# The end of the expert stage and the value products behind it: another list for the fillers, other engines for the copies, the taps of two batches moved among the output tiles

## The chip, the core and the metric

One core of a Trainium2 chip runs the whole program. The metric is device time in microseconds (us). A profile holds one execution, with the busy time of TensorE (PE for its matmuls, PEld for its weight loads), VectorE (DVE), ScalarE (ACT), GpSimd (POOL) and the DMA queue of SyncE (SP).

## The reference, cut to what matters

```python
# stage 1: attention, batch 4, 8 heads, 1152 positions, 64 wide, queries pooled by 2
x = softmax(pool(q) @ k.T / 8) @ v              # -> (4, 576, 512)
# stage 2: four experts, top 2 of 4, causal attention inside each
for e in range(4):
    y = softmax(causal(x @ wq[e] @ (x @ wk[e]).T / 8)) @ (x @ wv[e]) @ wo[e]
    out += (e among the top two) * gate_weight * y
# stage 3: a causal convolution of 5 taps makes the gate of a value product
gate_pre = sum(conv_w[k] * shifted(out, k) for k in range(5))
final = (sigmoid(gate_pre) * (out @ w_val)) @ w_out
```

All of it is float32. The kernel splits operands into a high and a low part in the matmul's reduced float32 format, so that a product is three matmuls: high by high, low weights by high, high weights by low.

## The kernel before

**Order.** All instructions are issued in an order written by hand; the engines run their own queues in order, and semaphores join them. Stage 2 is a loop over `n = 0..41`. Step `n` issues the scores of one tile (batch `b`, expert pair `g`, query block `i`, in the order i = 1, 3, 2, 4, 0, so that five steps make a pair and ten a batch). Two steps later (`LAG = 2`) the same tile's probabilities are transposed (`transp2`). A tile goes through: scores on PE (`scores2`), mask and row minimum on DVE, exponential on ACT (`expo2`), a reciprocal on DVE and a scaling on GpSimd (`norm2`, L850 or L855), transposes on PE, copies out of PSUM by `evac`. When the last tile of a pair is transposed, `av2` multiplies with the values; it is put at place 1 of the list `fill`.

**Fillers.** Between these, `pop` takes PE work from `fill`: projections of the next batch (`proj`, twelve matmuls), value and router products (`vgate`), output products of a batch (`mix`, six matmuls of 288 columns), and from n = 35 on fourteen of the sixteen value products of batches 0 and 1 (`raws`, six matmuls of 288 columns each, L779). How many are popped in a step follows from estimated costs and a `budget`. What a filler leaves for other engines is put on `late2` and issued at the next pop: for `raws` the copy out of PSUM, by `evac`. `evac` sends every other copy to ACT (L862) and to DVE (L864); its counter `turn` begins at 0 and serves `transp2` too, all through stage 2.

**Taps.** `mix` writes its rows to `x2` and, scaled with the last tap's weight, to `gp`, both on ACT (L937, L938). `conv` then hangs four taps a tile row on the list `rides`, DVE instructions of 576 columns (L215); each pop issues one, and each step one more, three a step at most (`room`).

**Behind the loop.** What is left of `fill` and the last two `raws` run, then `gate_all(0)` (sigmoids on ACT, L795, four multiplications on DVE, L1136), the eight `mix` halves of batch 3 with splits of the gated rows of batch 0 between them (`spread`, L790 on ACT and L791 on DVE), then the 18 output tiles `final(i, t)` of twelve matmuls (L1120): pair 0 is batches 0 and 1, pair 1 batches 2 and 3. `VF` says how many value products of batches 2 and 3 (`values`) follow each tile; each is multiplied with its gate on DVE (L1127) and split. `step` issues one entry, the leftovers of the one before and one or two taps.

**PSUM.** Projections, transposes, `mix`, `raws` and `av2` share four banks of `ps_m`. A bank comes free when its copy has run. Scores have two tiles of their own.

Of the kernel before, what the change touches and what calls it, by code (L numbers as in the profile page):

```python
# [12 lines left out]
AF = mybir.ActivationFunctionType  # L13
# [7 lines left out]
def tile_kernel(ctx, tc, q, k, v, w_gate, wq, wk, wv, wo, w_val, conv_w, w_out, wo_t, q0, k0, out):  # L21
# [751 lines left out]
    def value(yhs, b, m, hf, then):  # L773

        qsl = slice(hf * HQ, (hf + 1) * HQ)
        ps = ps_m.tile([P, 512], F32, name="a")
        ops = [(wi, yi, g) for g in range(EP) for wi, yi in THREE]
        for o, (wi, yi, g) in enumerate(ops):
            pe.matmul(ps[:, 0:HQ], lhsT=wf[:, g, wi, m * P:(m + 1) * P], rhs=yhs[b, g][:, yi, qsl], start=o == 0, stop=o == len(ops) - 1)  # L779
        late2.append(lambda: then(ps[:, 0:HQ], m, qsl))  # L780
# [16 lines left out]
    with ExitStack() as s2l:  # L797
# [56 lines left out]
                    dve.tensor_tensor(out=sm[rs, 0:1], in0=sm[rs, 0:1], in1=gw[rs, 4, 2 * g + e:2 * g + e + 1], op=ALU.mult)  # L854
                pool.tensor_tensor(out=p[:, 0:SQ], in0=p[:, 0:SQ], in1=sm[:, 0:1].to_broadcast([P, SQ]), op=ALU.mult)  # L855

        turn = [0]

        def evac(dst, src):
            turn[0] += 1  # L860
# [63 lines left out]
        def mix(b, yhs):  # L924

            box = {}

            def half(m, hf):
                if hf == 0:
                    box[m] = ((x2_p if m < 2 else x2b_p).tile([P, SQ], F32, name="x2"), o_p.tile([P, SQ], F32, name="gp")) if b < B - 1 else (end3["x2"][m], end3["gp"][m])  # L930
                x2, gp = box[m]
                qsl = slice(hf * HQ, (hf + 1) * HQ)
                ps = ps_m.tile([P, 512], F32, name="a")
                ops = [(wi, yi, g) for g in range(EP) for wi, yi in THREE]
                for o, (wi, yi, g) in enumerate(ops):
                    pe.matmul(ps[:, 0:HQ], lhsT=wos[wi][:, g, m * P:(m + 1) * P], rhs=yhs[g][:, yi, qsl], start=o == 0, stop=o == len(ops) - 1)
                act.activation(x2[:, qsl], ps[:, 0:HQ], AF.Copy)  # L937
                act.activation(gp[:, qsl], ps[:, 0:HQ], AF.Copy, scale=cw[:, m, KC - 1:KC])  # L938
                if hf == 1:
                    late2.append(lambda: rides.extend(conv(b, m, x2, gp)))  # L940

            return [(0.74, lambda m=m, hf=hf: half(m, hf)) for m in range(KT) for hf in range(2)]
# [7 lines left out]
            return steps  # L950

        VG, FD, IN, FL, PEND, PN = 5, 1, 1, 2.6, 7, 3
        GM, VF = (0, 1, 2, 3), (0, 0, 0, 3, 1, 2, 2, 2, 2, 2, 2)
        RD = (1, 0, 1, 1, 1)
        ORDER = (1, 3, 2, 4, 0)
        steps = [(b, g, i) for b in range(B) for g in range(EP) for i in ORDER]
        LAG = 2
        WORK = [(0.21, 0.22), (0.43, 0.44), (0.64, 0.65), (0.85, 0.87), (0.96, 0.55)]
# [37 lines left out]
        for n in range(len(steps) + LAG):  # L996
            if n < len(steps):
                b, g, i = s = steps[n]
                if n % 5 == 0:
                    pts[b, g] = (pt_p2.tile([P, 4, 2, SQ], F32, name="pt"), pt_p2.tile([R64, 2, R64], F32, name="pt4"))  # L1000
                    if g == 0 and b:
                        fill += proj(xh[b], 1, (lambda: xh.update({3: load2(3)})) if b == 2 else None)
                        if b == B - 1:
                            fill.append((0, lambda: late2.append(begin3)))
                    if n == 10 * B - 5:
                        buf = [f(c2.tile([P, 2, SQ], F32R, name=f"k20{i}")) for i in range(2)]
                        bufs = [c2.tile([P, SQ + R64], F32R, name=f"q20{i}") for i in range(2)]
                        v2 = v_p.tile([P, 5, ED + E], F32, name="v2").rearrange("p t c -> p (t c)")
                        first3["raw"] = [[buf[t // 2][:, t % 2] for t in range(KT)], [f(bufs[t])[:, 0:SQ] if t < 2 else v2[:, (t - 2) * SQ:(t - 1) * SQ] for t in range(KT)]]
                        raws = [(0.74, lambda i=i, m=m, hf=hf: value(yhs, i, m, hf, lambda ps, m, qsl: evac(first3["raw"][i][m][:, qsl], ps))) for i in range(2) for m in range(KT) for hf in range(2)]  # L1010
                        fill += raws[0:14]
                    if b == 0 and g == 1:
                        buf = y0_p.tile([P, EP, 2, SQ], F32R, name="y0")
                        yhs.update({(0, i): buf[:, i] for i in range(EP)})
                    if b == 1 and g == 0:
                        buf = y12_p.tile([P, 2, EP, 2, SQ], F32R, name="y12")
                        yhs.update({(1 + j, i): buf[:, j, i] for j in range(2) for i in range(EP)})
                if n % 10 == 5 and b + 1 < B:
                    fill += proj(xh[b + 1], 0)
                if n % 10 == VG and b + 1 < B:  # L1020
                    v2s[b + 1], gws[b + 1], vg = vgate(xh[b + 1])
                    fill += vg
                if n == 0:
                    fill += proj(xh[0], 1)
                if n == FD:
                    fill += [(2.6, lambda g=g: fold(g)) for g in range(EP)]
# [2 lines left out]
            own = [ahead(m) for m in range(n, n + left)]  # L1029
            budget = max(FL, (sum(c for c, _ in fill) + (PEND if 10 <= n and n % 10 < PN else 0) + sum(own)) / left) - own[0]  # L1030

            room = [3]

            def ride():
                if urgent:
# [19 lines left out]
                t += pop()  # L1055
            if n < len(steps):
                scores2(s)
            if fill:
                t += pop(RD[n % 5])
            else:  # L1060
                flush()
            if n >= LAG:
                b1, g1, i1 = steps[n - LAG]
# [8 lines left out]
                expo2(s)  # L1072
            if n == 0:
                flush()
            while fill and t < budget:
                t += pop()
            ride()
            if n == 9:
                xh[2] = load2(2)
            if n in (12, 22):  # L1080
# [13 lines left out]
                    rides.pop(0)()  # L1094

        CL = 2
        while len(fill) > 6:
            step(fill.pop(0)[1])
    s2.close()


    with ExitStack() as s3:
# [21 lines left out]
        def values(b, gp):  # L1124
            def then(ps, m, qsl):
                gt = gt_p.tile([P, HQ], F32, name="gt")
                dve.tensor_tensor(out=gt, in0=ps, in1=gp[m][:, qsl], op=ALU.mult)  # L1127
                spread(gt, gs[b // 2], m, b % 2 * SQ + qsl.start)

            return [(0.74, lambda m=m, hf=hf: value(yhs, b, m, hf, then)) for m in range(KT) for hf in range(2)]  # L1130

        def gate_all(i):
            sigm(first3["gp"][i])
# [5 lines left out]
        rest = values(2, gp2) + values(3, end3["gp"])  # L1139
        fin = [[(2.6, lambda i=i, t=t: final(i, t)) for t in range(9)] for i in range(2)]  # L1140
        mixs = mix(B - 1, [yhs[B - 1, g] for g in range(EP)])
        todo = fill + raws[14:] + [(0, lambda: gate_all(0))]
        for i in range(8):
            todo.append(mixs[i])
            if i in GM:
                todo.append(gates3.pop(0))
        for i in range(len(VF)):
            if i == 9:
                assert len(rest) <= 8
            todo.append((fin[0] + fin[1])[i])  # L1150
            if i == 0:
                todo.append((0, lambda: gate_all(1)))
                todo += gates3
            if i == 2:
                todo.append((0, lambda: sigm(gp2.values())))
            if i == 6:
                todo.append((0, lambda: sigm(end3["gp"].values())))
            todo += rest[0:VF[i]]
            del rest[0:VF[i]]
        assert not rest  # L1160
        for n, (_, a) in enumerate(todo + fin[1][len(VF) - 9:]):
            step(a, 1 + (n > 14))
        while late2:
            step(lambda: None)

# [43 lines left out]
```

## Time and profile before

| | us |
|---|---|
| median of three runs | 761.71 (761.33 to 763.0) |
| the profiled execution | 761.71 |
| its span, first to last instruction | 759.9 |
| PE, PEld, DVE, ACT, POOL busy | 745.7, 616.6, 569.4, 448.2, 316.3 |

The profiled execution is the median run, so 1.8 us lie outside the span. PE is busy for 98% of the span at the full granted clock. Matmuls overlap each other, so that a matmul that waits inside a row still counts as busy in part; the time from the start of one row to the start of the next tells more than the busy share.

### The profile page before, as it was taken

Reading aid. Unit: us, or ns where it says so; the run is one execution under the profiler, and the core shown is the slowest. Engines: PE = TensorE matmul, PEld = TensorE weight load, DVE = VectorE, ACT = ScalarE, POOL = GpSimd, SP = SyncE. Lnnn points to the kernel's source line nnn. Section 1 sums busy time; section 2 is a strip of 40 time slices with the busy share of each in tenths; the row PEclk is TensorE's granted clock in tenths of the full one; section 3 lists DMA queues with packets and bytes.
Section 4 is the critical chain, followed back from the end, with each engine's and each line's share of the span. In section 5 each row is a group of like instructions: output and inputs, shape, how many; then the busy total and the mean of one; then the engine's idle time right before and its main releaser. Section 6 shows DMA issues by size and latency. Waiting matters only on the chain.

```text
span 759.9 us, 14763 instructions
## 1 busy us (share of the span) xinstructions
PE 745.7 (98%) x5317; PEld 616.6 (81%) x5317; DVE 569.4 (75%) x1064; ACT 448.2 (59%) x985; POOL 316.3 (42%) x442
## 2 busy tenths in 40 slices
PE   8999999999999999999999999999999999999998
PEld 7787887787787787877878877988898888878887
DVE  6777888898888988756756766355889797988730
ACT  6665665665665756657656756334564654648632
POOL 6555675675676675652553501022322222220000
PEclk9999999999999999999999999999999999999999
DMA  7876878769778689666657581478425763800212
GB/s 258 254 174 203 226 190 255 211 195 261 209 227 250 187 262 258 178 204 208 166 164 227 132 286 48 111 210 189 135 54 141 199 159 81 267 1 15 84 57 97
DMA packets 83785, 133.52 MB, mean 176 GB/s; under 512 B 19072, under 2 KB 55424, under 8 KB 83712
## 3 DMA queue, kind: packets, MB, share of 16 engines
q1 hardware_dynamic: 83712, 132.58, 61.3%
q8 instruction: 42, 0.69, 0.4%
q14 instruction: 31, 0.25, 0.1%
HBM read 53.37 MB, written 21.76 MB: 99 GB/s over the span
## 4 chain that ended last, share of the span: by engine, by line
PE 84%; DVE 8%; DMA 3%; ACT 3%; issue 1%; SPq 0%; POOL 0%; POOLq 0%; ACTq 0%; DVEq 0%
PE s L440 21%; PE t L489 19%; PE t L519 18%; PE o L1120 7%; PE a L242 5%; PE a L275 4%; PE a L914 2%; DVE gp L215 2%; PE a L779 2%; PE s L814 2%; PE a L886 1%; DMA k<-hl 1%; PE t L478 1%; DVE nm L824 1%; DVE nm L445 1%
## 5 line engine op out<-in xcount | busy, mean ns | idle before, releaser
L452 ACT ACTIVATE p<-s,nm 128x1152 f32<-128x1152 f32 x144 | 176.2, 1223 | 87.9 <-DVE nm L445 85.8
L445 DVE TENSOR_REDUCE nm<-s 128x1 f32<-128x1152 f32 x144 | 192.1, 1352 | 13.9 <-PE s L440 13.6
L489 PE MATMUL t<-ident,p 128*128 128x128 f32 x1296 | 198.8, 275 | 0.7 <-DVE xf L521 0.4
L489 PEld LDWEIGHTS t<-ident,p 128*128 128x128 f32 x1296 | 149.1, 141 | 26.4 <-ACT pt L497 7.0
L497 ACT ACTIVATE pt<-t 128x384 f32<-128x384 f32 x223 | 102.1, 489 | 79.9 <-PE t L489 75.0
L519 PE MATMUL t<-pt,vn 128*64 128x256 f32 (+1 forms) x1152 | 146.7, 408 | 0.0
L499 DVE COPY pt<-t 128x384 f32<-128x384 f32 x209 | 110.9, 554 | 44.5 <-PE t L489 40.5
L519 PEld LDWEIGHTS t<-pt,vn 128*64 128x64 f32 x1152 | 80.0, 137 | 55.9 <-issue 5.2
L440 PE MATMUL s<-ka,qst 128*128 128x384 f32 x384 | 114.6, 380 | 0.2
L440 PE MATMUL s<-kb,qst 128*128 128x384 f32 x384 | 99.1, 367 | 1.7 <-ACT p L452 1.7
L850 POOL TENSOR_TENSOR p<-p,sm 128x512 f32<-128x512 f32 (+3 forms) x32 | 40.2, 1255 | 106.0 <-DVE sm L848 71.3
L440 PEld LDWEIGHTS s<-kb,qst 128*128 128x128 f32 x384 | 60.8, 189 | 15.7 <-issue 13.1
L440 PEld LDWEIGHTS s<-ka,qst 128*128 128x128 f32 x384 | 62.9, 190 | 1.1 <-DVE ka L574 0.9
L377 POOL TENSOR_TENSOR hlk<-kt,hlk 128x384 fp32r<-128x384 f32 x45 | 45.5, 1011 | 1.1
L521 DVE TENSOR_TENSOR xf<-t,rb 128x320 f32<-128x320 f32 (+1 forms) x32 | 14.6, 456 | 41.1 <-PE t L519 40.1
L467 POOL COPY rm<-rs 128x256 f32<-128x256 f32 x31 | 12.4, 401 | 79.3 <-DVE rs L462 77.7
L242 PE MATMUL a<-xh,wqk 128*128 128x288 f32 x288 | 43.3, 300 | 2.1 <-DVE pt L864 2.1
L835 ACT ACTIVATE p<-s,nm 128x256 f32<-128x256 f32 (+3 forms) x64 | 33.1, 524 | 20.3 <-DVE nm L824 20.3
L528 POOL CAST xt<-xf 128x320 fp32r<-128x320 f32 (+1 forms) x32 | 13.6, 426 | 69.9 <-DVE xf L521 69.3
L215 DVE SCALAR_TENSOR_TENSOR gp<-x,cw,gp 128x572 f32<-128x572 f32 (+3 forms) x48 | 40.4, 843 | 2.6 <-ACT gp L938 2.1
L242 PEld LDWEIGHTS a<-xh,wqk 128*128 128x128 f32 x288 | 39.4, 188 | 3.5 <-DVE pt L864 2.5
L440 PE MATMUL s<-hlk,mixed 128*128 128x384 f32 x135 | 33.7, 357 | 0.0
(193 smaller groups left out, 1170.8 us busy)
## 6 DMA issues: line engine op xcount, KB each, us to landing
ka<-hlk SPq DMA_DIRECT2D x90, 192.0 KB, 3.2
kb<-hlk SPq DMA_DIRECT2D x90, 192.0 KB, 3.7
vn<-in_v_dram SPq DMA_DIRECT2D x16, 576.0 KB, 7.2
k<-hl SPq DMA_DIRECT2D x32, 288.0 KB, 4.9
kt<-in_k_dram SPq DMA_DIRECT2D x15, 576.0 KB, 6.1
qt<-in_q_dram SPq DMA_DIRECT2D x15, 576.0 KB, 5.2
qst<-hlq SPq DMA_DIRECT2D x60, 128.0 KB, 3.2
xh<-x_d SPq DMA_DIRECT2D x12, 576.0 KB, 6.0
```

What stands on the lines that cost most here:

```text
L215: dve.scalar_tensor_tensor(out=gp[:, n:], in0=x[:, 0:SQ - n], scalar=cw[:, m, c:c + 1], in1=gp[:, n:], op0=ALU.mult, op1=ALU.add)
L242: pe.matmul(ps[:, 0:HQ], lhsT=wqk[wi][:, t, cs], rhs=xh[t][xi][:, qsl], start=o == 0, stop=o == len(ops) - 1)
L377: late.append(lambda: pool.tensor_tensor(out=hlk[:, 1, gs], in0=kt[:, gs], in1=f(hlk[:, 0, gs]), op=ALU.subtract))
L440: pe.matmul(ps[:, 0:GW], lhsT=ops[c][0], rhs=ops[c][1], start=c == 0, stop=c == len(ops) - 1)
L445: dve.tensor_reduce(d["nm"], d["s"][:, :, 0:GW], axis=AX.XY, op=ALU.min)
L452: act.activation(d["p"], d["s"][:, :, 0:GW], AF.Exp, bias=d["nm"], scale=-1.0, accum_out=sums[(2 * n + u) % len(sums)][:, i:i + 1])
L489: pe.transpose(ps[:, j * P:(j + 1) * P], p[:, g, j * P:(j + 1) * P], ident)
L497: act.activation(dst, src, AF.Copy)
L499: dve.tensor_copy(dst, src)
L519: pe.matmul(ps[64 * h:64 * h + 64, 0:N], lhsT=vn[:, h, j, :], rhs=pt[:, j, h, :], start=j == 0, stop=j == C - 1)
L850: pool.tensor_tensor(out=pv, in0=pv, in1=sm[:, :, None].to_broadcast([P, 2, w]), op=ALU.mult)
L1120: pe.matmul(ps[:, 0:w], lhsT=hl[xi][:, kt, t * P - a:(t + 1) * P - a], rhs=end3["wo3"][:, kt, wi, c:c + w], start=o == 0, stop=o == len(op ...
```

## The change

The counter `turn` begins at 1, which swaps ACT and DVE in every `transp2`. The copies of `raws` go to ACT alone. From n = 35 on the pops follow the fixed list `LAST`, and taps the list `TAPS` from n = 33 on (two in steps 33 and 34, one in 35 to 37, none in 38 to 40, four in 41), so that nine taps of batch 2 are left at the end of the loop, which now ends with `fill` empty. The last scaling of batch 3 (`gp`) is one GpSimd instruction a tile row instead of two of ACT. Behind the loop the taps are given out by entry: none at the `mix` halves, one at each of the first three output tiles, two at each later one; the taps of batch 3 run at the tiles 3 to 10. The value products come halves first; those of batch 2 follow the tiles 3 to 6, those of batch 3 follow tiles 11 and 12, four each. The sigmoids of batch 3 stand behind tile 10.

```diff
-        turn = [0]
+        turn = [1]
...
                 act.activation(x2[:, qsl], ps[:, 0:HQ], AF.Copy)
-                act.activation(gp[:, qsl], ps[:, 0:HQ], AF.Copy, scale=cw[:, m, KC - 1:KC])
+                if b < B - 1:
+                    act.activation(gp[:, qsl], ps[:, 0:HQ], AF.Copy, scale=cw[:, m, KC - 1:KC])
+                elif hf == 1:
+                    pool.tensor_scalar(gp, x2, cw[:, m, KC - 1:KC], None, op0=ALU.mult)
...
-        GM, VF = (0, 1, 2, 3), (0, 0, 0, 3, 1, 2, 2, 2, 2, 2, 2)
+        GM, VF = (0, 1, 2, 3), {3: 2, 4: 2, 5: 2, 6: 2, 11: 4, 12: 4}
...
+        LAST = {35: 2, 36: 2, 37: 1, 38: 1, 39: 1, 40: 1, 41: 2}
+        TAPS = {33: 2, 34: 2, 35: 1, 36: 1, 37: 1, 38: 0, 39: 0, 40: 0, 41: 4}
...
-                        raws = [(0.74, lambda i=i, m=m, hf=hf: value(yhs, i, m, hf, lambda ps, m, qsl: evac(first3["raw"][i][m][:, qsl], ps))) for i in range(2) for m in range(KT) for hf in range(2)]
+                        raws = [(0.74, lambda i=i, m=m, hf=hf: value(yhs, i, m, hf, lambda ps, m, qsl: act.activation(first3["raw"][i][m][:, qsl], ps, AF.Copy))) for i in range(2) for m in range(KT) for hf in range(2)]
...
-            room = [3]
+            room = [TAPS.get(n, 3)]
...
-            if fill:
-                t += pop(RD[n % 5])
-            else:
+            if fill and n < len(steps) + LAG - 1:
+                t += pop(RD[n % 5] and n not in LAST)
+            elif not fill:
                 flush()
...
-            while fill and t < budget:
+            while fill and t < budget and n not in LAST:
                 t += pop()
-            ride()
+            for _ in range(LAST.get(n, 0)):
+                pop(False)
+            for _ in range(max(1, TAPS.get(n, 1))):
+                ride()
...
-        while len(fill) > 6:
-            step(fill.pop(0)[1])
+        assert not fill
...
-            return [(0.74, lambda m=m, hf=hf: value(yhs, b, m, hf, then)) for m in range(KT) for hf in range(2)]
+            return [lambda m=m, hf=hf: value(yhs, b, m, hf, then) for hf in range(2) for m in range(KT)]
...
-        todo = fill + raws[14:] + [(0, lambda: gate_all(0))]
+        def gate_last(gps, left):
+            assert len(rides) <= left
+            sigm(gps.values())
+
+        todo = [(1, a) for _, a in raws[14:]] + [(0, lambda: gate_all(0))]
         for i in range(8):
-            todo.append(mixs[i])
+            todo.append((0, mixs[i][1]))
             if i in GM:
-                todo.append(gates3.pop(0))
-        for i in range(len(VF)):
-            if i == 9:
-                assert len(rest) <= 8
-            todo.append((fin[0] + fin[1])[i])
+                todo.append((0, gates3.pop(0)[1]))
+        for i, (_, a) in enumerate(fin[0] + fin[1]):
+            todo.append((1 if i < 3 else 2, a))
             if i == 0:
                 todo.append((0, lambda: gate_all(1)))
-                todo += gates3
+                todo += [(0, a) for _, a in gates3]
             if i == 2:
-                todo.append((0, lambda: sigm(gp2.values())))
-            if i == 6:
-                todo.append((0, lambda: sigm(end3["gp"].values())))
-            todo += rest[0:VF[i]]
-            del rest[0:VF[i]]
+                todo.append((0, lambda: gate_last(gp2, KT * (KC - 1))))
+            if i == 10:
+                todo.append((0, lambda: gate_last(end3["gp"], 0)))
+            todo += [(0, a) for a in rest[0:VF.get(i, 0)]]
+            del rest[0:VF.get(i, 0)]
         assert not rest
-        for n, (_, a) in enumerate(todo + fin[1][len(VF) - 9:]):
-            step(a, 1 + (n > 14))
+        for riders, a in todo:
+            step(a, riders)
```

## Rows read from the trace of the kernel before

**Rows 1.** Busy time by stretch: length, then each engine's busy us (instructions), clock, DMA.

```profile
631.22:653.78 22.56, 22.50 (x172) 20.32 (x170) 18.42 (x54) 13.41 (x41) 6.17 (x5) 1.00 0.62 164
653.78:684.32 30.54, 26.94 (x190) 21.38 (x188) 25.29 (x60) 14.40 (x42) 6.78 (x6) 1.00 0.26 94
684.32:693.84 9.52, 8.85 (x64) 8.15 (x61) 7.99 (x14) 8.96 (x24) 0.00 (x0) 1.00 0.01 2
693.84:756.98 63.14, 63.10 (x326) 53.61 (x324) 30.07 (x65) 28.78 (x66) 0.00 (x0) 1.00 0.19 72
```

**Rows 2.** PE in order of time: start, us, work, in brackets idle before it.

```profile
658.84 1.06 PE L779 MATMUL a<-y,wf 128*128 128x288 f32 x6 [1.07 <-DVE pt L864]
...
663.42 0.44 PE L901 MATMUL a<-pt,v 128*64 128x128 f32 x4 [0.78 <-DVE pt L864]
...
680.28 0.44 PE L886 MATMUL a<-ident,p 128*128 128x128 f32 x2 [0.47 <-POOL p L850]
681.33 0.44 PE L901 MATMUL a<-pt,v 128*64 128x128 f32 x4 [0.61 <-DVE pt L864]
...
684.32 1.86 PE L779 MATMUL a<-y,wf 128*128 128x288 f32 x12
```

**Rows 3.** DVE in order of time, two waits of PE.

```profile
658.10 0.68 DVE L864 COPY pt<-a 128x512 f32<-128x512 f32 x1
...
661.81 1.22 DVE L824 TENSOR_REDUCE nm<-s 128x2 f32<-128x1024 f32 x1
662.96 0.41 DVE L864 COPY pt<-a 128x256 f32<-128x256 f32 x1
```

**Rows 4.** DVE by line from 653.78 to 684.32: busy us, mean ns, idle before.

```profile
L215 DVE SCALAR_TENSOR_TENSOR gp<-x,cw,gp 128x575 f32<-128x575 f32 (+3 forms) x13 | 10.8, 836 | 0.1
...
L864 DVE COPY k<-a 128x288 f32<-128x288 f32 x4 | 1.8, 446 | 0.0
```

**Rows 5.** All engines in order of time, four PSUM banks and the last probability tile.

```profile
673.39 1.06 PE L779 MATMUL a<-y,wf 128*128 128x288 f32 x6 [0.25 <-ACT pt L862]
...
674.47 0.44 DVE L864 COPY q<-a 128x288 f32<-128x288 f32 x1
...
674.97 1.07 PE L779 MATMUL a<-y,wf 128*128 128x288 f32 x6
...
679.61 0.61 POOL L850 TENSOR_TENSOR p<-p,sm 128x256 f32<-128x256 f32 x1 [1.44 <-DVE sm L848]
```

**Rows 6.** ACT, then PE, at the last products of batch 3.

```profile
692.34 0.55 ACT L938 ACTIVATE pt<-a,cw 128x288 f32<-128x288 f32 x1
692.72 0.69 ACT L790 ACTIVATE wqk<-k 128x512 fp32r<-128x512 f32 x1
...
692.94 1.06 PE L936 MATMUL a<-hl,wos 128*128 128x288 f32 x6 [0.29 <-ACT pt L938]
```

**Rows 7.** PE among the output tiles, and DVE's gating of batch 1.

```profile
707.42 3.38 PE L1120 MATMUL o<-pt,wvg 128*128 128x512 f32 x12
...
735.97 1.75 PE L779 MATMUL a<-hl,wf 128*128 128x288 f32 x12
737.55 19.39 PE L1120 MATMUL o<-pt,gs 128*128 128x512 f32 x96
...
701.04 1.42 DVE L1136 TENSOR_TENSOR q<-q,xh 128x576 f32<-128x576 f32 x2
```

**Rows 8.** GpSimd: a one-input product by form; a scaling and a tap side by side.

```profile
L399 POOL TENSOR_SCALAR qp<-qp 128x576 f32<-128x576 f32 x15 | 24.7, 1650 | 1.3
...
652.12 1.15 POOL L855 TENSOR_TENSOR p<-p,sm 128x576 f32<-128x576 f32 x1 [3.83 <-ACT pt L862]
...
652.79 1.09 DVE L215 SCALAR_TENSOR_TENSOR gp<-x,cw,gp 128x575 f32<-128x575 f32 x1
```

**Rows 9.** PE and DVE at n = 32, the first output product of batch 2.

```profile
643.99 1.36 PE L936 MATMUL a<-y,wos 128*128 128x288 f32 x6
...
644.27 0.62 DVE L225 SCALAR_TENSOR_TENSOR y<-a,y 128x448 fp32r<-128x448 f32 x1 [0.82 <-ACT y L224]
```

## The prediction

> **What bounds the kernel now.** I read the table by engine first: PE is busy 98% of the span, so a change that leaves PE's work as it is can only win what PE stands still. The change moves no matmul in or out, so the question is where PE waits in the end of stage 2, and whether the new order waits elsewhere. I then cut the end into stretches [rows 1]: steps n = 30 to 34 (631.22 to 653.78), steps 35 to 41 (to 684.32), the last two value products and the eight `mix` halves (to 693.84), and the 18 output tiles. Last I read PE, DVE and ACT in order of time where PE stops [rows 2, 3, 5, 6].
>
> PE's busy column hides most of it, because a waiting matmul overlaps its neighbours. So I count starts against work. Twelve matmuls of 288 columns go from 735.97 to 737.55 [rows 7], 0.79 us for six. In steps 30 to 34 there are 96 of them by the code (four projections, eight `mix` halves): 12.6 of 22.56 us. The other 9.9 are five scores, five sets of transposes and one `av2`. Steps 35 to 41 hold the same scores, seven sets of transposes, two `av2` and fourteen value products: 9.9, plus a second `av2` of 2.99 (681.33 to 684.32, [rows 2]), plus two small sets of transposes (I take 0.6; their rows allow up to 1.5, since a pair shows 0.44 with its overlap), plus 14 x 0.79 = 11.1, together 24.6 us. They took 30.54, so PE stood 5.9 us (5.0 at least). In the `mix` stretch ten units of 0.79 are 7.9 of 9.52: 1.6 us stood. The tiles: seven in 19.39 us [rows 7], 2.77 each, 18 of them and sixteen value products of 0.79 make 62.5 of 63.14: 0.6 stood. At most 8.1 us can be won there.
>
> What PE waits for: at 658.84 a bank of PSUM that DVE empties only from 658.10 on, at 663.42 a copy for `av2` that DVE does behind a row minimum of 1.22 us [rows 2, 3]; then the scaling of the last tile and its copy on DVE (680.28, 681.33). These four rows show 2.9 us of idle; the rest lies inside rows, as at 674.97, which starts just when DVE's copy of 674.47 is through, while at 673.39 a bank that ACT empties was taken at once [rows 5]. The common cause is DVE: 25.3 busy in 30.5 us [rows 1], 10.8 of them taps and about 3.1 (seven at 0.446) copies of value products [rows 4], all in one queue ahead of minima and evacuations. ACT is busy 14.4.
>
> **The change part by part.**
>
> *Taps in steps 33 to 41.* Following the lists through the code, the old loop issues ten taps of batch 2 in steps 35 to 38, the new one three in 35 to 37 and four in 41. Six to seven taps of 0.836 [rows 4], 5 to 6 us, leave DVE's queue ahead of the minima. With the copies below it falls from 25.3 to about 17 us busy in a stretch of some 25.
>
> *Value copies on ACT.* Seven copies leave DVE (3.1 us) and go to ACT. Each costs ACT at most the 0.55 of the scaled copy of equal size [rows 6], 3.9 us on top of 14.4 in 25 to 30: hidden behind PE's matmuls. Queued behind them are exponentials; without this cover one copy would cost its 0.55.
>
> *Evacuations swapped.* In a pair ACT now takes the block of 512 for i = 4 and the last block, i = 0, those which PE waited for at 658.84 and 663.42. DVE takes i = 1. That hurts at n = 32: DVE would copy 512 columns (0.68 as in [rows 3]) between the transposes and the low part of `y` at 644.27, for which the product at 643.99 already waits (1.36 instead of 0.79, [rows 9]). I take +0.35, between 0 and 0.68. In batches 1 and 2 the `mix` comes a step later by the code and the low part is ready. The other PSUM waits of stage 2 stay, since a pair still has one DVE copy at the same place in DVE's queue.
>
> *Order of pops.* Two value products a step, and one ahead of each `av2`, give PE 0.79 us of work while the last copy runs: this covers the 0.78 and 0.61 of [rows 2]. The last tile's chain: from 674.97, just behind its scores, to the end of its scaling at 680.22 are 5.25 us [rows 5], in which DVE's queue held a tap and three value copies (2.2 us) that are gone: about 3.1. PE has four value products and two sets of transposes in between, 3.2 + 1.2 = 4.4 us. It should hold, with 1.3 us to spare for handovers. Of the 5.9 us I keep 0.8 (bounds 0 and 3.0, half of it): **-5.1**.
>
> *Four taps at n = 41* stand ahead of the low part of the last `y`. From the start of `av2`: 0.4, four taps 3.3, the low part 0.62 [rows 9], so ready at 4.4; the first `mix` half wants it at 2.99 + 1.58 + 0.66 = 5.2. Hidden, with 0.8 to spare.
>
> *The `mix` stretch.* Eight scaled copies (4.4 us of ACT at 0.55) go. The last half waited for exactly such a copy [rows 6], with ACT 8.96 busy of 9.52 [rows 1]; now ACT has eight plain copies and four splits there, about 6 us, and DVE no taps between its multiplications. What takes its place: DVE starts the multiplications after two more taps, at 4.4 + 1.7 = 6.1 from the start of `av2`, four take 2.84 (two in 1.42, [rows 7]), and each split follows its own. The splits on ACT then pace the last halves, close to PE's own 0.79. Of 1.6 I keep 0.5 (bounds 0 and 1.6): **-1.1**.
>
> *GpSimd's four products.* A product with a constant of 128x576 takes 1.65 us there [rows 8], so 6.6 in all, on an engine that is idle in that stretch [rows 1]. The first user, a tap of batch 3, comes behind tile 3, 11 us on: hidden, and if that cover were gone 1.65 a row. No DMA is added or moved past another; SP issues the same stores, and the load of the last weights stays hung on the first `av2`.
>
> *Output tiles.* The stall at 707.42 (3.38 for a tile, [rows 7]) came from splits of batch 1, late because the gating at 701.04 stood behind taps. With one tap instead of about ten ahead of it this goes: **-0.5** of 0.6 (bounds 0 and 0.6). DVE's new load up to the value products of batch 3: 19 taps of 0.81 to 0.84 (16), the gating 2.8, splits of batch 1 about 3.6, and sixteen instructions of 288 columns at 0.45 (7.2): near 30 us in 11 tiles and eight products, 36.8 us. Head-of-line waits for an ACT copy at each tile's end cost some; my walk through the order leaves DVE about 2 us early for the sigmoids behind tile 10, and those some 5 us early for tile 13. Batch 3's products in fours fill all four banks, and the multiplications free them within a tile.
>
> Sum: 5.1 + 1.1 + 0.5 - 0.35 = 6.4 us less. The profiled execution is the median, 761.7: **755.3 us**. With the bounds (3.0 kept and nothing from the other two, 0.68 lost; or everything won) this case gives 753.6 to 759.5, most of it below 757.5; the 9.9 us of steps 30 to 34 hold the wait of [rows 9] themselves, 0.57 us, so a little more could be won than I count.
>
> **The rivals.**
>
> *The attention chain takes over.* With DVE eased, PE reaches the transposes sooner, and minimum, exponential, reciprocal and scaling of the last three tiles follow each other; the margin of 1.3 us is small against seven handovers. For it: PE waited on GpSimd at 680.28 though it was slow. Against: 2.2 us leave that chain. If half or more of the 5.9 us stays and the rest of the sum halves: about 758.5 us.
>
> *GpSimd slows DVE.* A tap that ran beside a GpSimd product of two inputs for 0.48 us took 1.09 instead of 0.81, 0.28 more [rows 8], or 0.58 for each shared microsecond. The four products fall where DVE multiplies and splits batch 0: up to 6.6 x 0.58 = 3.8 us there. The first tile's last operand is ready some 1.5 us before its use by my walk, so up to 2.3 us would show: 757.2 us. Against it: the product has one tensor input, and only part of it lies beside DVE's work. The Trainium skill, "GPSIMD Engine Reference", Key points, says that both engines share SBUF interfaces and that instructions of DVE with two SBUF inputs contend; the row agrees for GpSimd's two-input form, and none shows it for the form with one.
>
> *The work only moves.* The taps taken out of steps 35 to 38 stop PE at the tiles by as much as they freed: 761.7. DVE's load of 30 in 36.8 us speaks against it.
>
> *Slower.* Batch 3's taps end late, the sigmoids wait, and with them the products and tile 13. DVE has about 7 us before PE stops there, and 6.4 more before the gain is gone: 13.4 us late. Nineteen taps all at 1.09 would be 5.3. If the walk is wrong by more, 764.
>
> **How the numbers follow.** The forecast 0.62, the chain 0.20, GpSimd's contention 0.08, moved work 0.06, slower 0.04. Differences under 0.2%, 1.5 us, can't be told from none. The range 752.8 to 759.4 holds the forecast, the contention and three quarters of the chain: 0.8 and a little. Faster: the first three, less 0.01 of the chain near 760.2: 0.89; same 0.07; slower 0.04.
>
> **What would show it.** In the profile after: steps 35 to 41 in about 25.5 us with DVE near 17 busy; no wait of PE on DVE's copies there; the `mix` stretch near 8.4 us with ACT less than full; the tiles in 62.6; taps up to tile 10 and the sigmoids of batch 3 done before tile 11 ends. Wrong would be: transposes of the last pair waiting for GpSimd, the first tile waiting for a low part, or gaps of PE ahead of tiles 12 to 14.

## The result, and the profile after

The changed kernel takes 754.54 us (median of six, 753.9 to 757.84) against 761.67 for the one before (six, 761.33 to 763.89): 0.9909 of its time, interval 0.9894 to 0.9924. The forecast was 755.3 in 752.8 to 759.4.

The profiled execution is the longest of the six, 757.84 us with a span of 755.7: in it PE waited for a transfer in steps 25 to 29 and then ran at a lower granted clock, which its other stretches don't show, nor do four of the six executions (mean granted clock 1.0). Busy time by stretch of the kernel after: length, each engine's busy us (instructions), clock, DMA. The rows are steps 25 to 29, 30 to 34, 35 to 41, the last two value products with the `mix` halves, and the tiles; the last four answer to [rows 1].

```profile
605.01:633.98 28.97, 26.65 (x184) 23.81 (x183) 22.93 (x51) 13.60 (x42) 6.49 (x6) 0.88 0.45 125
633.98:657.13 23.15, 22.50 (x171) 20.31 (x170) 18.41 (x56) 14.25 (x44) 6.17 (x5) 1.00 0.63 167
657.13:681.95 24.82, 24.82 (x190) 20.99 (x189) 17.09 (x45) 15.78 (x46) 6.78 (x6) 1.00 0.30 110
681.95:690.21 8.26, 8.26 (x65) 8.12 (x61) 8.22 (x16) 8.01 (x22) 2.79 (x1) 1.00 0.01 2
690.21:752.74 62.53, 62.49 (x326) 53.85 (x324) 35.43 (x69) 27.41 (x61) 9.12 (x4) 1.00 0.19 73
```

In the third and fourth row PE is busy for the whole stretch. The list of PE's waits is empty from 657.13 on; from 500 us to the end of the kernel after it holds three entries (engine, line, waited for: us, times, longest):

```profile
PE a L242 <- DVE pt L864: 1.6, 2, 0.8
PE a L242 <- DMA xh<-x_d: 1.5, 2, 0.8
PE a L936 <- DVE y L225: 0.7, 1, 0.7
```

Lengths of the same stretches in all profiles, from the start of the scores of one step to the next (us; blank where the rows of a run don't bound a stretch):

| | 15–19 | 20–24 | 25–29 | 30–34 | 35–41 | `mix` | tiles |
|---|---|---|---|---|---|---|---|
| before | 24.36 | 22.63 | 24.60 | 22.56 | 30.54 | 9.52 | 63.14 |
| after | 24.16 | 22.25 | 28.97 | 23.15 | 24.82 | 8.26 | 62.53 |
| turn 0 (e1) | 24.36 | 22.64 | 25.61 | 22.56 | 25.48 | 8.26 | 62.53 |
| value copies shared (e2) | 24.16 | 22.25 | 25.04 | 23.15 | 25.50 | 8.26 | 62.53 |
| taps early (e3) | 24.16 | 22.25 | 27.59 | 23.15 | 30.04 | 8.25 | 62.56 |
| `gp` on ACT (e4) | 24.17 | 22.24 | 25.51 | 23.15 | 24.81 | 9.81 | 62.56 |
| before, with copies on ACT (e5) | 24.36 | 22.64 | 24.56 | 22.56 | 29.08 | 9.81 | 63.15 |
| before, with taps moved (e6) | 24.40 | 22.63 | 24.55 | 22.55 | 27.18 | 9.51 | 68.04 |
| constant on GpSimd (e7) | 24.17 | 22.24 | 25.58 | 23.15 | 24.81 | 8.26 | 62.54 |
| one block always on ACT (e8) | 25.45 | 21.84 | 25.60 | 22.56 | 25.10 | 8.25 | 62.54 |
| more taps at the tiles (e9) | 24.16 | 22.25 | 25.22 | 23.16 | 24.81 | 8.24 | 62.56 |
| load from GpSimd (e10) | 24.17 | | | 23.15 | 24.80 | 8.26 | 62.54 |
| order mended, load from GpSimd (e11) | 23.31 | | | 22.56 | 24.81 | 8.26 | 62.53 |
| order mended (e12) | 23.31 | 22.24 | 29.22 | 22.56 | 24.81 | 8.24 | 62.56 |

PE in order of time in the kernel after, where [rows 2] showed waits ahead of the last transposes and the last `av2`:

```profile
676.93 1.06 PE L779 MATMUL a<-y,wf 128*128 128x288 f32 x6
677.82 0.40 PE L886 MATMUL a<-ident,p 128*128 128x128 f32 x2
677.98 1.05 PE L779 MATMUL a<-y,wf 128*128 128x288 f32 x6
678.95 0.44 PE L901 MATMUL a<-pt,v 128*64 128x128 f32 x4
...
681.95 1.86 PE L779 MATMUL a<-y,wf 128*128 128x288 f32 x12
683.65 6.72 PE L936 MATMUL a<-hl,wos 128*128 128x288 f32 x48
```

No bracket is left: a value product lies ahead of the transposes and another ahead of `av2`, and the 48 `mix` matmuls follow each other without a gap, where the last six waited for ACT in [rows 6]. DVE by line in steps 35 to 41 of the kernel after (busy us, mean ns, idle before), beside [rows 4]:

```profile
L215 DVE SCALAR_TENSOR_TENSOR gp<-x,cw,gp 128x575 f32<-128x575 f32 (+3 forms) x7 | 5.6, 806 | 0.0
...
L864 DVE COPY pt<-a 64x128 f32<-64x128 f32 (+2 forms) x5 | 2.5, 494 | 0.2
```

Seven taps where there were thirteen, and L864 holds copies of transposes alone. All engines at the last tile's chain:

```profile
672.70 0.68 DVE L864 COPY pt<-a 128x512 f32<-128x512 f32 x1
...
672.87 0.74 ACT L837 ACTIVATE p<-s,nm 128x576 f32<-128x576 f32 x1 [0.52 <-DVE nm L826]
...
673.11 1.01 PE L779 MATMUL a<-y,wf 128*128 128x288 f32 x6
...
673.74 0.15 DVE L844 TENSOR_SCALAR sm<-sm 128x1 f32<-128x1 f32 x1 [0.36 <-ACT p L837]
...
674.48 0.43 DVE L823 TENSOR_TENSOR s<-s,cmask 128x256 f32<-128x256 f32 x1
...
677.11 0.61 POOL L850 TENSOR_TENSOR p<-p,sm 128x256 f32<-128x256 f32 x1 [1.35 <-DVE sm L848]
```

The scaling ends at 677.72 and the transposes begin at 677.82: the chain holds with 0.1 us to spare, not 1.3. From 673.11, just behind its scores, it takes 4.61 us where the forecast had 3.1. The mask begins only at 674.48, because DVE's queue first copies 512 columns and then waits for the exponential of the tile before it. The value products and transposes on PE last just as long.

At n = 32, PE and then DVE of the kernel after, beside [rows 9]:

```profile
646.74 0.90 PE L936 MATMUL a<-y,wos 128*128 128x288 f32 x5
648.30 0.40 PE L936 MATMUL a<-y,wos 128*128 128x288 f32 x1 [0.65 <-DVE y L225]
```
```profile
647.02 0.69 DVE L864 COPY pt<-a 128x512 f32<-128x512 f32 x1 [0.75 <-PE a L886]
647.63 0.61 DVE L225 SCALAR_TENSOR_TENSOR y<-a,y 128x448 fp32r<-128x448 f32 x1
```

This is the loss that was forecast: the copy of 512 columns stands ahead of the low part, and steps 30 to 34 are 0.59 us longer.

### The profile page after: what moved, and what is told of

It is laid out like the page before. It is cut to its first block, busy times and chain, and to the rows that moved or that the text cites. A ratio compares the mean times of both kernels' runs of the same rounds, so it can differ in the third digit from the quotient of the medians.

```text
span 755.7 us, 14760 instructions
## 1 busy us (share of the span) xinstructions
PE 744.6 (99%) x5317; PEld 618.9 (82%) x5317; DVE 566.3 (75%) x1056; ACT 447.7 (59%) x985; POOL 328.3 (43%) x446
## 4 chain that ended last, share of the span: by engine, by line
PE 93%; DVE 3%; DMA 2%; ACT 1%; issue 0%; SPq 0%; ACTq 0%
PE s L440 21%; PE t L489 19%; PE t L519 19%; PE a L242 7%; PE o L1127 7%; PE a L275 4%; PE a L779 3%; PE a L914 3%; PE s L814 3%; PE a L886 2%; PE a L936 2%; PE t L478 1%; DMA xh<-x_d 1%; PE s L821 1%; DVE nm L445 1%; PE a L770 1%
## 5 line engine op out<-in xcount | busy, mean ns | idle before, releaser
L242 PE MATMUL a<-xh,wqk 128*128 128x288 f32 x288 | 45.6, 309 | 3.1 <-DVE pt L864 1.6
L242 PEld LDWEIGHTS a<-xh,wqk 128*128 128x128 f32 x288 | 41.1, 195 | 4.9 <-DVE pt L864 2.0
```

The source lines that it names most:

```text
L242: pe.matmul(ps[:, 0:HQ], lhsT=wqk[wi][:, t, cs], rhs=xh[t][xi][:, qsl], start=o == 0, stop=o == len(ops) - 1)
```

## The experiments

**Which part carries steps 35 to 41: four runs.** The first undoes the swap of ACT and DVE alone (e1).

```diff
-        turn = [1]
+        turn = [0]
```

> The changed kernel with the counter of the copies back at 0, so that the transposed blocks go to ScalarE and VectorE as they did before. Theory 1 (VectorE's queue was the cause, and the new lists empty it): with a light queue it does not matter which engine takes a block; PE gets back the 0.6 us at n = 32 and loses a few tenths in steps 35 to 41: 753.9 to 754.8 us, steps 35 to 41 at 24.8 to 25.5. Theory 2 (the swap did it, since the copies that PE waits for left VectorE): the waits ahead of av2 and at the bank of i = 4 come back, 1.07 + 0.78 + 0.61: 756.5 to 757.5 us, steps 35 to 41 near 27.3.

755.91 us, ratio to before 0.9923 (0.9909 to 0.9938). Steps 35 to 41 are 0.66 us longer than after, steps 30 to 34 0.59 shorter: near the end the swap gains and loses nearly the same. The median lies between the ranges of the two theories; 25.48 us for steps 35 to 41 is what the first one expected. The swap acts earlier in stage 2 too, where the forecast took it to change nothing: with it, steps 10 to 14 take 22.30 us instead of 22.70, and steps 15 to 19 and 20 to 24 are 0.20 and 0.38 shorter. In PE's rows, the output product behind the transposes of step 14 starts 0.95 us after these in e1 (556.15, 557.10) and 0.58 us after them in the kernel after (555.54, 556.12), and the same pair of step 24 lies 0.95 and 0.57 apart; the first projection of step 15 waits 1.06 us for DVE's copy in e1 and 0.82 in the kernel after.

The second gives the copies of value products back to both engines (e2).

```diff
-  ... value(yhs, i, m, hf, lambda ps, m, qsl: act.activation(first3["raw"][i][m][:, qsl], ps, AF.Copy))
+  ... value(yhs, i, m, hf, lambda ps, m, qsl: evac(first3["raw"][i][m][:, qsl], ps))
```

> The changed kernel, but the copies of the value products alternate between ScalarE and VectorE again. Theory 1: VectorE has 3 us more in steps 35 to 41, still far from full: 0.3 to 1.5 us slower than the changed kernel, 754.8 to 756.0. Rival (the copies are the larger half of the cause, since each holds one of four banks): half of the 5.7 us comes back, 757 to 758.

754.9 us, 0.9917 (0.9902 to 0.9932); steps 35 to 41 take 25.50. Within the change the copies are worth 0.7 us.

The third lets the taps ride as before, one a pop and one a step, with the pops of `LAST` (e3).

```diff
-            room = [TAPS.get(n, 3)]
+            room = [3]
...
-                t += pop(RD[n % 5] and n not in LAST)
+                t += pop(RD[n % 5])
...
-                pop(False)
-            for _ in range(max(1, TAPS.get(n, 1))):
+                pop()
+            for _ in range(1):
```

> The changed kernel, but the taps of batch 2 run in steps 33 to 41 as before, up to three a step. Theory 1: the taps are the larger part of VectorE's queue, so 2 to 4 us of PE's waits come back in steps 35 to 41: 756.5 to 758.5. Rival (copies and the order of the pops did it): within 0.5 us of the changed kernel, 754.0 to 755.0.

760.71 us (twelve runs), 0.9981 (0.9969 to 0.9994). Steps 35 to 41 are back at 30.04, while the `mix` stretch and the tiles keep their gain. PE's waits there, and DVE's taps, in this run:

```profile
PE a L886 <- ACT k L1015: 2.1, 1, 2.1
PE a L779 <- DVE hl L225: 0.8, 1, 0.8
```
```profile
L215 DVE SCALAR_TENSOR_TENSOR gp<-x,cw,gp 128x572 f32<-128x572 f32 (+3 forms) x12 | 9.7, 814 | 0.1
```

Twelve taps instead of seven bring 5.22 of the 5.72 us back. The way from a tap to PE leads over ACT here: two taps (from 671.52, 1.66 us) stand ahead of the mask and the row minimum of one tile, ACT waits 2.62 us for that minimum before the tile's exponential at 675.40, and the value copies behind the exponential empty the bank that PE waits for.

Not all of the 5.22 is waiting. The granted clock was 0.94 over this stretch and 0.55 from 678.00 to 681.80, behind the wait of 2.1: an estimate from this row is that 1.7 us (45% of 3.8) are the clock, so some 3.5 are the taps. The two of the twelve executions with a mean granted clock of 1.0 say much the same: they took 757.92 and 758.08 us, some 3.5 above the median of the kernel after and within the expected 756.5 to 758.5, which the median of all twelve misses.

The fourth returns the last scaled copies to ACT (e4).

```diff
-                if b < B - 1:
-                    act.activation(gp[:, qsl], ps[:, 0:HQ], AF.Copy, scale=cw[:, m, KC - 1:KC])
-                elif hf == 1:
-                    pool.tensor_scalar(gp, x2, cw[:, m, KC - 1:KC], None, op0=ALU.mult)
+                act.activation(gp[:, qsl], ps[:, 0:HQ], AF.Copy, scale=cw[:, m, KC - 1:KC])
```

> The changed kernel, but the last scaled copies of batch 3 run on ScalarE again, eight of them. Theory 1: ScalarE is full in the stretch of the mix halves again, and they take 9.2 to 9.5 us instead of 8.3: 755.4 to 755.8. Rival (GpSimd's products, now 3.0 us each, slow VectorE by sharing the memory ports): VectorE's multiplications shrink and the whole is no slower, 754.0 to 754.6.

756.66 us, 0.9935 (0.9919 to 0.9951). The `mix` stretch takes 9.81 against 8.26, and PE waits for ACT again, as in [rows 6]; its `mix` halves in this run:

```profile
686.74 1.06 PE L936 MATMUL a<-hl,wos 128*128 128x288 f32 x6 [0.29 <-ACT pt L938]
688.09 1.07 PE L936 MATMUL a<-hl,wos 128*128 128x288 f32 x6 [0.29 <-ACT pt L938]
```

The products on GpSimd are the whole gain of that stretch; the loss without them is larger than expected (9.2 to 9.5).

**The two main parts by themselves, on the kernel before.** The copies alone (e5, the line of e2 the other way round):

> The kernel before with another part of the change alone: the copies of the value products all on ScalarE. Theory (VectorE's queue as a whole is the cause, so each part that leaves it counts): 3.1 us leave it, steps 35 to 41 take 28.0 to 29.8 instead of 30.54: 759.3 to 761.0. Rival (taps fill what is freed, or the taps alone hold PE up): within 0.4 us of the kernel before.

760.8 us (eleven runs), 0.999 (0.9981 to 0.9999). Steps 35 to 41 gain 1.46, and the `mix` stretch loses 0.29.

The taps alone (e6): only `TAPS` and `room`, with the old pops and the old list behind the loop.

```diff
+        TAPS = {33: 2, 34: 2, 35: 1, 36: 1, 37: 1, 38: 0, 39: 0, 40: 0, 41: 4}
...
-            room = [3]
+            room = [TAPS.get(n, 3)]
```

> The kernel before with one part of the change alone: the list of taps for steps 33 to 41. Copies, engines, pops and tiles are as before, so that the taps left over run at one an entry behind the loop, among the mix halves. Theory (the taps in VectorE's queue are the larger part of PE's waits): steps 35 to 41 take 26.0 to 27.5 instead of 30.54 us, and a part is given back in the mix stretch, where VectorE has nine more taps: 757.0 to 759.0 in all. Rival (it needs copies, engines and pops together): steps 35 to 41 stay above 29, 760.5 to 762.

763.94 us, 1.0031 (1.0019 to 1.0044): slower than before, and outside both expected ranges. Steps 35 to 41 gain 3.36, and the tiles lose 4.90: 3.1 us are waits, and behind them the granted clock falls too, to a mean of 0.97 over the tiles. PE's wait among the tiles, and DVE in order of time at the first of them, in this run:

```profile
PE o L1121 <- DVE wqk L791: 3.1, 3, 1.4
```
```profile
692.28 1.66 DVE L215 SCALAR_TENSOR_TENSOR pt<-pt,cw 128x572 f32<-128x572 f32 x2
693.85 0.69 DVE L791 TENSOR_TENSOR wqk<-k,wqk 128x512 fp32r<-128x512 f32 x1
694.45 0.22 DVE L791 TENSOR_TENSOR wvg<-k,wvg 128x64 fp32r<-128x64 f32 x1
694.59 1.67 DVE L215 SCALAR_TENSOR_TENSOR pt<-pt,cw 128x574 f32<-128x574 f32 x2
```

This is the rival "the work only moves", come true: without the new list of taps by entry the taps that are left, and those of batch 3 behind them, fall between the splits of batch 0, and the first tile waits for its low parts.

**What GpSimd's products cost.** A constant 0.5 in place of the weights (e7, one execution):

```diff
-                    pool.tensor_scalar(gp, x2, cw[:, m, KC - 1:KC], None, op0=ALU.mult)
+                    pool.tensor_scalar(gp, x2, 0.5, None, op0=ALU.mult)
```

> The changed kernel, with GpSimd's last scaling by the constant 0.5 instead of the taps' weights, so that this part of the computation is another one. The four products took 2.98 us each in the changed kernel and 1.65 was forecast from a product with a constant. If the operand makes the difference they take 1.65 again; if it is VectorE's work beside them they stay near 3.0. The time is that of the changed kernel in both cases.

754.4 us. GpSimd in the kernel after, then with the constant:

```profile
687.42 11.91 POOL L941 TENSOR_SCALAR pt<-pt,cw 128x576 f32<-128x576 f32 x4 [9.69 <-ACT pt L937]
```
```profile
683.98 9.99 POOL L941 TENSOR_SCALAR pt<-pt 128x576 f32<-128x576 f32 x4 [9.68 <-ACT pt L937]
```

A product takes 2.98 us with the weights (11.91 / 4) and 2.50 with the constant, against 1.65 in [rows 8]: the operand is worth 0.48, and the other 0.85 stays with the constant too. DVE's multiplications and first splits of batch 1 in the kernel after, and then in e4, where GpSimd does nothing there:

```profile
694.45 1.43 DVE L1143 TENSOR_TENSOR q<-q,xh 128x576 f32<-128x576 f32 x2 [2.92 <-ACT xh L795]
695.79 1.89 DVE L1143 TENSOR_TENSOR v<-v,xh 128x576 f32<-128x576 f32 x2
697.61 0.88 DVE L791 TENSOR_TENSOR wvg<-q,wvg 128x64 fp32r<-128x64 f32 x2
```
```profile
693.25 1.43 DVE L1140 TENSOR_TENSOR q<-q,xh 128x576 f32<-128x576 f32 x2 [3.11 <-ACT xh L795]
694.60 1.42 DVE L1140 TENSOR_TENSOR v<-v,xh 128x576 f32<-128x576 f32 x2
695.94 0.42 DVE L791 TENSOR_TENSOR wvg<-q,wvg 128x64 fp32r<-128x64 f32 x2
```

Beside GpSimd's products DVE is held up at two places, by 0.47 and 0.46 us, and not elsewhere in the 11.9 us that they share. In e7, where the products lie at other times, the places are others too: a tap at 687.30 takes 1.21 us instead of 0.81, and the pair of multiplications again 1.89. None of it reaches PE: `mix` stretch and tiles are equal in after and e7, and the tiles are no shorter in e4 without the products (62.56).

**How much room DVE has at the tiles.** Sixteen more taps of 576 columns, one behind each tap of batch 3, into a row that nothing reads any more (e9, one execution):

```diff
+            if b == B - 1:
+                steps = [lambda a=a: (a(), tap(first3["gp"][0][m], x2, m, 0)) for a in steps]
```

> The changed kernel with sixteen further taps of 0.8 us on VectorE, one behind each tap of batch 3, into memory that nothing reads any more: 13 us more of VectorE among the tiles 3 to 10. It measures the room there. The forecast's walk (2.4 us early for the sigmoids in the trace, about 5 more before tile 13 waits): the tiles take 5 to 6 us longer, 68 instead of 62.5. Rival (PE depends on the sigmoids sooner, since the products in fours hold all four banks): 8 to 11 us longer. If VectorE had much more room than thought: under 2 us.

754.82 us, tiles of 62.56: the expected loss didn't come. The tiles' row of this run:

```profile
687.53:750.09 62.56, 62.52 (x326) 53.86 (x324) 45.88 (x85) 26.84 (x62) 9.13 (x4) 1.00 0.20 73
```

DVE is busy for 10.45 us more. Part of it fills time in which DVE stood waiting for ACT before its splits (7.4 us in the kernel after, 3.0 here); the last tap of batch 3 ends 42.1 us behind the first tile's start instead of 35.1, and PE doesn't notice. The room is at least 7 us.

**Two tries at a better version.** The loss at n = 32 can go if the single first block always goes to ACT; and one `mix` half was left for n = 15 and 25 (e8).

```diff
-        def evac(dst, src):
-            turn[0] += 1
-            if turn[0] % 2:
+        def evac(dst, src, first=True):
+            if first:
...
-            while fill and t < budget and n not in LAST:
+            while fill and t < budget and n not in LAST and not (n in (14, 24) and len(fill) == 1):
```

> The changed kernel with two repairs of what it left or made: single transposed blocks (i = 1 and i = 0) all go to ScalarE, of each pair the first to ScalarE and the second to VectorE, so that the low part of y at n = 32 is not held up; and steps 14 and 24 leave one mix half for the next step, so that the projection at n = 15 and 25 comes 0.8 us later, behind VectorE's copy and the load of x. Theory: steps 30 to 34 back to 22.6 (0.6 less), 0.4 to 0.8 less at each of n = 15 and 25: 752.2 to 753.4. Rival (ScalarE's longer queue delays the exponentials): 754 to 755.5.

754.51 us, 0.9907 (0.9893 to 0.992): equal to the change, as its rival expected. Steps 30 to 34 are back at 22.56, but 35 to 41 lose 0.28 and steps 15 to 19 lose 1.29 against the change. Not all of the 1.29 is a loss, since the `mix` half that was left is work of step 14: steps 10 to 14 are 0.40 shorter (21.90).

The second try moves only the block of n = 32 to ACT and takes taps out of the ends of batches 0 and 1, with the load of `x` for batch 3 issued from GpSimd (e11) or left on SP (e12); the load alone is e10.

```diff
-            if turn[0] % 2:
+            if turn[0] % 2 or turn[0] == 50:
...
-        TAPS = {33: 2, 34: 2, 35: 1, ...
+        TAPS = {13: 2, 14: 2, 23: 2, 24: 2, 33: 2, 34: 2, 35: 1, ...
...
-   ... xh.update({3: load2(3)}) ...
+   ... xh.update({3: load2(3, nc.gpsimd)}) ...
```

> The changed kernel with the load of batch 3's x issued from GpSimd's queue instead of SyncE's, where it stands behind ten moves of keys and queries. It tests what the changed kernel waits for at n = 25, since PE comes there 0.6 us sooner after the load's issue than before. If it is the late issue, the load starts 3 to 4 us sooner, the wait (0.6 to 1.5 us) and the fall of the clock behind it go, steps 25 to 29 take 24.3 to 24.6 us, and the median is 753.2 to 754.0 with less spread. If it is bandwidth shared with the moves, nothing changes or the scores of n = 25 wait for the moves: 754.3 to 756.

> Both together: the two repairs and the load of x from GpSimd's queue. If all of it holds the wait at n = 25 goes too: 752.0 to 753.0. If the load's queue does not matter it is equal to the kernel with the two repairs.

> The changed kernel with two repairs: the block i = 1 of n = 32 alone goes to ScalarE, and steps 13, 14, 23, 24 issue at most two taps, as 33 and 34 do in the change. Theory: steps 30 to 34 back to 22.6 (0.6 less) and the 0.8 us of PE behind VectorE's copy at n = 15 goes; at n = 25 the load of x takes its place: 752.8 to 753.6. Rival (the wait at 15 is for something that the taps don't delay): 753.8 to 754.2.

| | us | ratio to before |
|---|---|---|
| e10 load from GpSimd | 755.55 | 0.9919 (0.9905 to 0.9932) |
| e11 order mended, load from GpSimd | 759.32 | 0.9967 (0.9955 to 0.9978) |
| e12 order mended, load on SP | 756.12 | 0.9925 (0.9912 to 0.9938) |

None of the three brought what it was made for; of e10 the rival came true, since the scores of n = 25 wait for the moves. The mended order shortens its own stretches (15 to 19 in 23.31, 30 to 34 in 22.56), yet the median of e12 lies 1.6 us behind the change, though their intervals overlap. The time goes in steps 25 to 29: 29.22 us, the only stretch of e12 that is longer than before. All five executions of e12 have a mean granted clock under 1.0 (0.995 to 0.998), where the kernel after has two in six. The wait of PE in e12, and PE in e11:

```profile
PE a L242 <- DMA xh<-x_d: 2.2, 3, 0.8
```
```profile
609.20 0.79 PE L814 MATMUL s<-k,q 128*128 128x256 f32 x2 [4.59 <-DMA q<-hl]
```

With the load on GpSimd's queue the wait for `xh` is gone, and PE waits for `q` instead: its transfers are late in its place. The median landing of its 128 KB parts goes from 4.9 us in the kernel after to 8.7 in e10 and 10.7 in e11, and steps 20 to 29 together take 48.09 us in e10 and 53.87 in e11, against 47.23 before.

**The transfer at n = 25.** The first projection of batch 3 reads `xh`, loaded by SP shortly before. From five profiles of kernels with the same load: the time from SP's issue of the load to that projection's start, the median time from issue to landing, and PE's wait.

| | issue to projection | issue to landing | wait of PE |
|---|---|---|---|
| before | 8.00 | 5.5 | none |
| after | 7.38 | 7.4 | 1.5 |
| e1 | 8.15 | 7.3 | 0.8 |
| e2 | 7.34 | 5.5 | 0.6 |
| e12 | 4.38 | 5.6 | 2.2 |

Two things bring the wait: PE comes sooner behind the issue (e2, e12), and the load lands later (after, e1). With 8 us and a landing in 5.5 there is none. In e12 the issue itself is late, at 601.00 against 599.08 in the kernel after: the mended order put a store (`g_d`, at 594.80) ahead of it in SP's queue. Why the landing varies stays open: e1 has the order of the kernel before up to there, and lands late too.

## Why the prediction was right, step by step

**Right in its mechanism.** DVE's queue was the common cause: the taps put back bring back 5.22 of 5.72 us (e3), some 3.5 of it without the clock, and 3.36 were gained by the taps alone on the kernel before (e6). DVE is busy 17.1 of 24.8 us; "near 17 in some 25" was forecast. The taps and the copies don't add up to the whole (3.36 and 1.46 on the kernel before, e6 and e5, 4.82 together); the swap adds 0.66 (e1), and what the new list of pops is worth alone no run shows. The forecast did not split the term between them.

**The terms of the sum**, forecast and measured in the table of stretches:

| | forecast | measured |
|---|---|---|
| steps 35 to 41 | -5.1 (0.8 kept of 5.9) | -5.72 |
| `mix` stretch | -1.1 (0.5 kept of 1.6) | -1.26 |
| tiles | -0.5 (of 0.6) | -0.61 |
| n = 32 | +0.35 (0 to 0.68) | +0.59 |
| sum | -6.35 | -7.00 |

Each is within its bounds, the tiles at theirs. What was kept back for waits was kept for little: PE's stretches hold none. The loss at n = 32 came out near its upper end, where the copy of 0.69 us stands wholly ahead of the low part.

**Too sure:** "the other PSUM waits of stage 2 stay". The swap takes 0.40, 0.20 and 0.38 out of steps 10 to 24 (e1), 1.0 in all. The kernel after reaches step 25 1.6 us earlier (605.01 against 606.62 before), but the other 0.6 lie ahead of step 10 and can't be told from the spread there: step 10 begins at 536.30 in the kernel after, at 536.93 before, and at 537.39 in e9, which has the same order. The load at n = 25, which the forecast didn't look at, takes a part back: steps 25 to 29 are 0.4 to 1.0 longer than before in e2, e4, e7 and e9, which have the order of after up to there. So -7.00 and -1.0 and +0.4 to 1.0, and 0.3 more outside the span (757.84 less 755.7, against 761.71 less 759.9), make 6.7 to 7.3 us less; the medians are 7.13 apart. That the forecast lies only 0.8 from the median is owed in part to two omissions of opposite sign.

**The last tile's chain** held, as forecast, but on 0.1 us and not 1.3: 4.61 us instead of 3.1. The step that failed is the walk from taps and copies taken out of DVE's queue to a shorter chain. What is late next in that queue, the exponential of the tile before, was not counted. The first rival was closer than its working made it.

**The four taps at n = 41:** nine taps of batch 2 were left behind step 40; with these four, five were left at the end of the loop, not nine. The low part of the last `y` was to be ready 4.4 us behind the start of `av2`. DVE in order of time in the kernel after:

```profile
679.96 3.24 DVE L215 SCALAR_TENSOR_TENSOR gp<-x,cw,gp 128x575 f32<-128x575 f32 x4
683.11 0.62 DVE L225 SCALAR_TENSOR_TENSOR hl<-a,hl 128x448 fp32r<-128x448 f32 x1
```

It was ready at 683.73, 4.78 behind 678.95, 0.08 into the first `mix` half, and PE doesn't wait. The multiplications begin at 685.09, 6.14 behind it; 6.1 was forecast.

**GpSimd's products** were sized at 1.65 us and take 2.98; the end of the four moves from about 694 (687.42 and 6.6) to 699.33. The cover named for them holds: the first user, a tap of batch 3 behind tile 3, runs at 702.87. The rival that they slow DVE is seen in its rows, 0.9 us where its working had up to 3.8, and costs PE nothing. (By its own figures, 755.3 and up to 2.3, its time goes up to 757.6, not 757.2.)

The Trainium skill, "GPSIMD Engine Reference", section Key points, says that the two engines share SBUF interfaces and that instructions of DVE with two SBUF inputs contend; the trace agrees now for the form with one tensor input as well, by the rows of after and e4 (1.89 us beside 1.42). The Trainium skill, "GPSIMD Engine Reference", section Engine selection, calls one-input work on GpSimd "roughly line-rate"; the rows differ, with 1.65, 2.50 and 2.98 us where a DVE tap of as many columns with two tensor inputs takes 0.81, and they decide.

**The tiles:** DVE's load was put at 30 us and its room at about 7; e9 shows that 7 us of delay cost nothing. The sigmoids of batch 3 were to end before tile 11 does. ACT, then PE of the kernel after:

```profile
727.68 2.39 ACT L795 ACTIVATE pt<-pt 128x576 f32<-128x576 f32 x4
```
```profile
729.65 3.32 PE L779 MATMUL a<-hl,wf 128*128 128x288 f32 x24
```

DVE's taps end at 725.31, 2.4 us ahead of the sigmoids (about 2 forecast); the sigmoids end 0.4 behind the tile, and only DVE's multiplications wait for the products, as they would anyway.

**Work that only moves** is real for another version: e6 moves the taps without a place for them and comes out at 1.0031. Of the slower rival, late taps of batch 3, nothing was seen, even with e9's load.

## What to carry to other kernels

Work that an engine off the path does for later can hold the path by its place in the queue alone: here moving taps some steps later was worth about 3.5 us (e3, e6), and only together with a new place for them, since moved alone they stopped PE elsewhere (e6). After taking entries out of a queue, walk it again for what is late next: the chain that was to gain 2.2 us gained 0.6. And a gain made ahead of a transfer that is issued just in time is partly lost there; issuing the load from another queue only moved the wait to other transfers (e10, e11).

## What the runs showed of the hardware that was not expected

TensorE's granted clock fell after three short waits, the last two of them for a transfer. PE in order of time in the kernel after, then windows of 3 us from 606 on (clock after PE, PEld, DVE, ACT, POOL):

```profile
606.46 1.10 PE L242 MATMUL a<-xh,wqk 128*128 128x288 f32 x6 [0.82 <-DVE pt L864]
608.36 0.71 PE L242 MATMUL a<-xh,wqk 128*128 128x288 f32 x3 [0.80 <-DMA xh<-x_d]
609.78 1.09 PE L242 MATMUL a<-xh,wqk 128*128 128x288 f32 x3 [0.71 <-DMA xh<-x_d]
```
```profile
606.00:609.00 3.00, 1.74 (x9) 1.29 (x9) 2.90 (x8) 1.91 (x6) 0.61 (x1) 0.97 0.72 287
609.00:612.00 3.00, 2.29 (x11) 2.17 (x11) 0.42 (x2) 0.66 (x2) 0.00 (x0) 0.50 0.03 10
612.00:615.00 3.00, 3.00 (x13) 2.94 (x13) 2.59 (x7) 1.42 (x6) 0.14 (x1) 0.50 0.00 0
```

Three gaps of 0.7 to 0.8 us, 2.3 together, and the granted clock is at 0.50, the 1.2 GHz level, for the next 6 us, in which PE is busy again. The stretch is 4.4 us longer than before, of which the waits for the transfer are 1.5; PE's busy time grows by 3.1 (26.65 against 23.54 before). In e2, with a gap of 0.82 and one of 0.60, the clock stayed at 1.00 and the stretch was 0.44 longer: the clock, not the wait, is most of the price. In e3 (0.82, 0.55, 0.76) and in e12 (0.69, 0.78, 0.74) the clock fell at this place as well; in e1, e4, e7 and e9, which have two gaps there, the second of 0.74 to 0.76, it stayed at 1.00. The other surprise was the spread of one GpSimd instruction on 128x576, 1.65 to 2.98 us: 0.48 of it is the operand (e7), and what brings the other 0.85 was not tried.
